# Batch zero by halves, dummy matmuls in the first gaps, folded weights in pairs of chunks, and the softmax scale moved into the input

## The chip, the cores and the metric

The kernel runs on one core of a Trainium2 chip. The metric is the device time of one execution in microseconds (us), median of several runs. The engines of the core run side by side and meet at semaphores: TensorE (PE, matmuls; PEld is its weight load), VectorE (DVE), ScalarE (ACT), GpSimd (POOL, which here also issues the loads) and SyncE (SP, which issues the stores).

## The reference

Two attentions in a row, and then a two-layer network with a squared ReLU. The shapes are 8 batches, 8 heads, 576 tokens, 32 packed queries, head size 64; the network has width 512 and an inner width of 2048.

```python
def sm_attn(qq, kk, vv):
    s = scale * np.matmul(qq, kk.transpose(0, 1, 3, 2))     # scale = 1/8
    s = s - np.max(s, axis=-1, keepdims=True)
    a = np.exp(s)
    a = a / (np.sum(a, axis=-1, keepdims=True) + 1e-09)
    return np.matmul(a, vv)
p_packed = sm_attn(p, k, v)             # 32 packed queries read 576 tokens
out = sm_attn(q, p_packed, p_packed)    # 576 tokens read the 32 packed results
x = out.transpose(0, 2, 1, 3).reshape(B * S, H * D)
h = x @ w_in
g = np.maximum(h, 0.0) ** 2
return g @ w_out                        # 4608 x 512, float32
```

## The kernel before

The kernel never forms `x`. It multiplies the packed result `pp` of a batch by `w_in` once, which gives a folded weight `M` of 2 x 128 rows (two groups `qd` of four heads, 32 packed entries each) by 2048 columns. Layer one then is `M` times the normalised weights `a2` of the second attention. The steps of one batch, by their names in the plan:

| step | what it does |
|---|---|
| Lk, Lv, Lq | loads of keys, values, queries, cast to bf16 on the way (issued by GpSimd) |
| Tk, Tq | transposes on VectorE |
| S1, PV | scores and context of the packed queries; XT copies them out (`pp`, `rD` = 1/denominator, `pq`) |
| M | folded weights, four chunks of 512 columns |
| S2, N | scores of the second attention, exponential, sum, log, inverse, product (`a2`) |
| R | layer one and ReLU, 16 blocks of 128 of the inner width |
| F1 | square (into `gT`); F2 | layer two, in tiles of 128 tokens |

A list scheduler in the kernel (`Plan`) puts the steps of all batches in an order at build time, with a time for each piece and a count of buffers for each pool. Each engine runs its instructions in that order. The parts that matter here (cuts are marked):

```python
    def fills(self, gap, t):          # dummy matmuls for a planned gap of TensorE
        return 0
...
        def keep_clock(ps):
            for _ in range(plan.fill):
                nc.tensor.matmul(ps, lhsT=idle_b[:, :P], rhs=idle_b, start=True, stop=True)
...
            def dma_kq(self, name, qd):       # all of one group's keys or queries
                t = getattr(self, name + "b")[qd] = qkv.tile([P, JT * D], BF16, name=name + "_b", tag="kqb")
                nc.gpsimd.dma_start(t, src[self.b, qd * QH:(qd + 1) * QH].rearrange("h (a j) d -> (h a) (j d)", j=JT))
            def tr_q(self, qd):
                nc.vector.transpose(
                    self.qT[:, qd].rearrange("p dh (j a) -> p j dh a", a=32),
                    self.t.qb[qd][:].rearrange("p (j dh dl) -> p j dh dl", dh=2, dl=32))
...
            def m(self, c):
                pss = [ps_att.tile([P, 512], F32, name="ps_a", tag="a") for _ in range(NQD)]
                keep_clock(pss[0][:, :256])
                for h in range(QH):
                    for qd in range(NQD):
                        pr, e = divmod(h, 2)
                        o = 32 * (h ^ qd)
                        nc.tensor.matmul(pss[qd][o:o + 32, :], lhsT=self.pp[64 * e:64 * e + 64, qd * P + pr * 64 + 32 * (e ^ qd):][:, :32],
                                         rhs=w_in_b[64 * e:64 * e + 64, qd * 2 + pr, c * WCH:(c + 1) * WCH], start=True, stop=True)
            def m_out(self, c, e, eng):
                if eng is nc.scalar:
                    nc.scalar.activation(dst, self.psm[c][e], ACT.Copy, scale=self.rD[:, e:e + 1])
                else:
                    nc.vector.tensor_scalar_mul(dst, self.psm[c][e], self.rD[:, e:e + 1])
...
            def n_mul(self, qd, hf):
                nc.vector.tensor_tensor(out=self.a2[:, qd, n0:n1].rearrange("p (c n) -> p c n", n=HALF),
                                        in0=self.e2[qd, hf], in1=self.ls[qd, hf], op=ALU.mult)
...
        def f1_mm(a, fb):
            ps = ph[a.b, fb] = ps_h.tile([P, 2, 512], F32, name="ps_h", tag="h")
            for qd in range(NQD):
                for c in range(2):
                    nc.tensor.matmul(ps[:, c, :HALF], lhsT=a.M[:, qd, fb * FB:(fb + 1) * FB],
                                     rhs=a.a2[:, qd, c * HALF:(c + 1) * HALF], start=(qd == 0), stop=(qd == NQD - 1))
...
        WIDE = tuple(range(B))      # batches whose second attention runs on all 576 tokens at once
        ld = load_steps(0) + w_in_load() + w_out_load()[:2] + load_steps(1) + w_out_load()[2:]
```

PSUM has three pools of two tiles each: `ps_a` (one bank a tile: S1, PV, M), `ps_h` (two banks a tile: S2, N, layer one) and `ps_o` (layer two).

Of the kernel before, what the change touches and what calls it, by code (L numbers as in the profile page):

```python
# [10 lines left out]
ALU = mybir.AluOpType  # L11
# [37 lines left out]
class Plan:  # L49
# [232 lines left out]
        return best[1]  # L282

    def fills(self, gap, t):
        return 0


def kernel_impl(tc, q, k, v, p, w_in, w_out, out):
# [15 lines left out]
    with ExitStack() as ctx:  # L304
# [4 lines left out]
        att = ctx.enter_context(tc.tile_pool(name="att", bufs=2))  # L309
        small = ctx.enter_context(tc.tile_pool(name="small", bufs=3))  # L310
        mpool = ctx.enter_context(tc.tile_pool(name="mpool", bufs=2))
        rpool = ctx.enter_context(tc.tile_pool(name="rpool", bufs=3))
        opool = ctx.enter_context(tc.tile_pool(name="opool", bufs=3))
        ps_att = ctx.enter_context(tc.tile_pool(name="ps_att", bufs=2, space=bass.MemoryType.PSUM))
        ps_h = ctx.enter_context(tc.tile_pool(name="ps_h", bufs=2, space=bass.MemoryType.PSUM))
# [34 lines left out]
                eng.tensor_copy(dst, src)  # L350

        def setup():
            nc.vector.memset(pT_bd[0][:, :BDW + 2 * P], 0.0)
            nc.vector.memset(ones_c[:, :1], 8.0)
            nc.vector.memset(ones_c[:64, 1:2], 8.0)
            nc.vector.memset(ones_c[64:, 1:2], 0.0)
            nc.vector.memset(kT[:, :, GM * P + 64:], 0.0)
            nc.vector.memset(v_t[0][64:, :, GM * D:], 0.0)
            nc.vector.memset(v_t[1][64:, :, GM * D:], 0.0)
            nc.vector.memset(pq_bd[0][:, :BDW + 2 * P], 0.0)  # L360

        def setup_rest():
            nc.gpsimd.memset(ones_bd, 0.0)
            for h in range(QH):
                nc.gpsimd.memset(ones_bd[32 * h:32 * h + 32, 32 * h:32 * h + 32], 0.125)
            nc.gpsimd.memset(pT_bd[1][:, :BDW + 2 * P], 0.0)
            nc.gpsimd.memset(pq_bd[1][:, :BDW + 2 * P], 0.0)
            nc.gpsimd.memset(idle_b, 0.0)

        def keep_clock(ps):  # L370
            for _ in range(plan.fill):
# [25 lines left out]
        class Loads:  # L397
# [5 lines left out]
            def dma_kq(self, name, qd):  # L403
                src = {"k": k, "q": q}[name]
                t = getattr(self, name + "b")[qd] = qkv.tile([P, JT * D], BF16, name=name + "_b", tag="kqb")
                nc.gpsimd.dma_start(t, src[self.b, qd * QH:(qd + 1) * QH].rearrange("h (a j) d -> (h a) (j d)", j=JT))  # L406

            def dma_v(self, i, h0, h1):
                n = GM + 1 if i < 2 else GM
                src = v[self.b, h0:h1].rearrange("h (a j) d -> a h (j d)", j=JT)  # L410
                nc.gpsimd.dma_start(self.vr[32 * i:32 * i + 32, h0:h1, :n * D], src[:, :, J0[i] * D:(J0[i] + n) * D])  # L411
# [13 lines left out]
        class Att:  # L425
# [8 lines left out]
                    setattr(self, name, pool.tile(shape, dt, name=name, **kw))  # L434
                return getattr(self, name)

            def tr_q(self, qd):
                self.tile_of("qT", att, [P, NQD, 2, S], BF16, bufs=1)
                nc.vector.transpose(  # L439
                    self.qT[:, qd].rearrange("p dh (j a) -> p j dh a", a=32),  # L440
                    self.t.qb[qd][:].rearrange("p (j dh dl) -> p j dh dl", dh=2, dl=32))

            def tr_k(self, qd):
                for i, n in (0, GM + 1), (2, GM):
# [68 lines left out]

            def m(self, c):
                self.tile_of("M", mpool, [P, NQD, DFF], BF16)
                pss = [ps_att.tile([P, 512], F32, name="ps_a", tag="a") for _ in range(NQD)]
                keep_clock(pss[0][:, :256])
                for h in range(QH):
                    for qd in range(NQD):
                        pr, e = divmod(h, 2)  # L520
                        o = 32 * (h ^ qd)
                        nc.tensor.matmul(pss[qd][o:o + 32, :], lhsT=self.pp[64 * e:64 * e + 64, qd * P + pr * 64 + 32 * (e ^ qd):][:, :32],  # L522
                                         rhs=w_in_b[64 * e:64 * e + 64, qd * 2 + pr, c * WCH:(c + 1) * WCH],
                                         start=True, stop=True)
                self.psm[c] = pss

            def m_out(self, c, e, eng):
                dst = self.M[:, e, c * WCH:(c + 1) * WCH]
                if eng is nc.scalar:
                    nc.scalar.activation(dst, self.psm[c][e], ACT.Copy, scale=self.rD[:, e:e + 1])  # L530
                else:
                    nc.vector.tensor_scalar_mul(dst, self.psm[c][e], self.rD[:, e:e + 1])  # L532

            def ps_s(self, hf):
                if hf is None:
# [38 lines left out]
            def n_mul(self, qd, hf):  # L574
                self.tile_of("a2", att, [P, NQD, S], BF16)
                n0 = 0 if hf is None else hf * HALF
                n1 = S if hf is None else n0 + HALF
                nc.vector.tensor_tensor(out=self.a2[:, qd, n0:n1].rearrange("p (c n) -> p c n", n=HALF),  # L578
                                        in0=self.e2[qd, hf], in1=self.ls[qd, hf], op=ALU.mult)

        gT = consts.tile([P, NFB, 2 * S], BF16, name="gT")

# [2 lines left out]
        def f1_mm(a, fb):  # L585
            ps = ph[a.b, fb] = ps_h.tile([P, 2, 512], F32, name="ps_h", tag="h")
            keep_clock(ps[:, 0, :256])
            for qd in range(NQD):
                for c in range(2):
                    nc.tensor.matmul(ps[:, c, :HALF], lhsT=a.M[:, qd, fb * FB:(fb + 1) * FB],  # L590
                                     rhs=a.a2[:, qd, c * HALF:(c + 1) * HALF],
                                     start=(qd == 0), stop=(qd == NQD - 1))

        def f1_relu(a, fb, eng):
            if (a.b, fb // 2) not in rr:
# [56 lines left out]
        def cast_alt(n, engs, fn):  # L652
            return [(NAME[id(e)], COST[NAME[id(e)]][0] + n * COST[NAME[id(e)]][1] / 1000, lambda e=e: fn(e)) for e in engs]

        plan = Plan({"a": 2, "h": 2, "o": 2, "dl": 8, "p": 1, "pb": 2, "kqb": NKQ, "v": 2, "e2": 3, "r": 3,
                     "osb": 3, "ls": 2})


# [5 lines left out]
        def stage(*pieces):  # L664
            return list(pieces)
# [5 lines left out]
        def load_steps(b):  # L671
            def kq(nm, qd):
                return load_step(f"L{nm}.{b}.{qd}", 0.56, 1.5, lambda: L[b].dma_kq(nm, qd), [("kqb", 1)])

            def vv(p, n):
                h0, h1 = p * H // n, (p + 1) * H // n
                return [load_step(f"Lv.{b}.{p}.{i}", 0.6, (0.82 if i < 2 else 0.66) / n,
                                  lambda i=i: L[b].dma_v(i, h0, h1), [("v", 1)] if p == 0 and i == 0 else [])
                        for i in range(4)]

            return [kq("k", 0), kq("k", 1)] + vv(0, 1) + [kq("q", 0), kq("q", 1)]

        def w_in_load():
# [11 lines left out]
        def tr_steps(b, nm):  # L695
            if b == 0:
                old = []
            elif nm == "k":
                old = [f"S1.{b - 1}.{i}" for i in range(3)]
            else:  # L700
                old = [f"S2.{b - 1}.{qd}.{hf}" for qd, hf in halves(b - 1)]
            us = 0.84 if nm == "k" else 1.37
            return [Step(f"T{nm}.{b}.{qd}", [stage([("DVE", us, lambda qd=qd: (T[b].tr_k if nm == "k" else T[b].tr_q)(qd))])],
                         [f"L{nm}.{b}.{qd}"] + old, (), [("kqb", 0, f"L{nm}.{b}.{qd}")]) for qd in QDS]

# [21 lines left out]
                         [f"PV.{b}.1"], (), [("a", 2, f"PV.{b}.0")])]  # L727

        def m_steps(b):
            return [Step(f"M.{b}.{c}",  # L730
                         [stage([("PE", 0.43, lambda c=c: T[b].m(c))]),
                          stage(*[[("ACT", 0.69, lambda c=c, e=e: T[b].m_out(c, e, A)),
                                   ("DVE", 0.74, lambda c=c, e=e: T[b].m_out(c, e, V))] for e in QDS])],
                         [f"XT.{b}/2.0"] + [f"LWI.{c}.{i}" for i in range(2)], [("a", 2)], [("a", 1, None)])
                    for c in range(NWC)]

        def halves(b):
            return [(qd, None) for qd in QDS] if b in WIDE else QH2

        def s2_steps(b):  # L740
            res = []
# [2 lines left out]
            for qd, hf in halves(b):  # L744
                res.append(Step(f"S2.{b}.{qd}.{hf}",
                                [stage([("PE", 0.26 * m, lambda qd=qd, hf=hf: T[b].s2(qd, hf))]),
                                 stage([("ACT", 0.73 if wide else 0.49, lambda qd=qd, hf=hf: T[b].s2_exp(qd, hf))])],
                                [f"XT.{b}/2.{i}" for i in range(3)] + [f"Tq.{b}.{qd}"] + (["Z"] if b == 0 else []),
                                [(pool, 1), ("e2", 1)], [(pool, 1, None)]))
                res.append(Step(f"N.{b}.{qd}.{hf}",  # L750
                                [stage([("PE", 0.13 * m, lambda qd=qd, hf=hf: T[b].n_sum(qd, hf))]),
# [8 lines left out]

        def f1_steps(b):
            res = []
            for fb in range(NFB):
                st = [stage([("PE", 0.49, lambda fb=fb: f1_mm(T[b], fb))]),
                      stage([("ACT", 0.65, lambda fb=fb: f1_relu(T[b], fb, A))]
                            + ([("DVE", 0.75, lambda fb=fb: f1_relu(T[b], fb, V))] if b < NDV else []))]
                deps = [f"M.{b}.{fb // 4}"] + [f"N.{b}.{qd}.{hf}" for qd, hf in halves(b)]
                res.append(Step(f"R.{b}.{fb}", st, deps, [("h", 1)] + ([("r", 1)] if fb % 2 == 0 else []), [("h", 1, None)]))
            return res

# [64 lines left out]
                        [f"LP.{b0}"], [("pb", 1)], [("p", 0, f"LP.{b0}"), ("pb", 1, None)])  # L835

        NDV = 1
        NB_ACTQ = -1
        WIDE = tuple(range(B))
        ROUNDS = 1  # L840
        SEEDS = ()
        setup()
        plan.base.update(DVE=2.5, POOL=0.8, ACT=0.5, SP=0.3, DMA=1.2, PE=3.6)
        plan.stream(0, [pload(0, 2)])
        ld = load_steps(0) + w_in_load() + w_out_load()[:2] + load_steps(1) + w_out_load()[2:]
        for b in range(2, B):
            ld += load_steps(b)[:2] + ([pload(2, B)] if b == 2 else []) + load_steps(b)[2:]
        plan.stream(0, ld)
        plan.stream(0.5, [Step("Z", [stage([("POOL", 2.6, setup_rest)])], ["Lq.0.1/1.0"])])
        plan.stream(1, [pprep(0, 2), pprep(2, B)])  # L850
        plan.stream(3.5, sum([v_steps(b) for b in range(B)], []))
        plan.stream(1.5, [x_step(b) for b in range(B)])
# [55 lines left out]
```

The softmax here doesn't subtract the row's maximum and nothing guards it: scores larger than these inputs give would overflow.

## Time and profile before

| | |
|---|---|
| time, median of 3 | 255.87 us (255.71 to 257.02) |
| profiled execution | span 255.2 us |
| first matmul of the kernel | 7.00 us |
| last matmul, about | 251.4 us |
| TensorE waits for v_b (context of batch 0) | 1.4 us |
| TensorE waits for pq_bd (scores of batch 0) | 3.2 us |
| TensorE waits for w_out_b loads | 1.0 us |
| TensorE waits for pT_bd on GpSimd | 0.9 us |

How to read it: the busy shares of the page say which engine may be the bound, the stages say where it stands idle, and the timeline and the chain of waits say for what. [...]

### The profile page before, as it was taken

What the parts mean: (1) busy time and instruction counts of PE and PEld (TensorE: products, weight loads), DVE (VectorE), ACT (ScalarE), POOL (GpSimd) and SP (SyncE); (2) the same over time, 40 slices, a digit from 0 to 9 for tenths busy, and PEclk for the clock granted to TensorE, in tenths of its full rate; (3) what the DMA queues carried; (4) which work ended last, traced back from release to release, by engine and by line L of the source; (5) the groups of instructions that cost most, each with busy time, mean ns of one, the idle gap of its engine ahead of it and who ended that gap; (6) DMA issues with size and microseconds to landing.
All of it is one profiled execution on the core that took longest, in us unless ns stands there. A gap on an engine that the chain in (4) does not pass through costs nothing.

```text
span 255.2 us, 4833 instructions
## 1 busy us (share of the span) xinstructions
PE 235.5 (92%) x1856; PEld 136.5 (53%) x1856; DVE 147.1 (58%) x260; ACT 158.4 (62%) x281; POOL 58.9 (23%) x121
## 2 busy tenths in 40 slices
PE   0647998989999999999999999999999999999994
PEld 0523664565565575467436763567446645644453
DVE  5557897879989977787675768453345304500000
ACT  2237887778789778578856876677746734611110
POOL 7884563487442055103000000000000000000000
PEclk9997999999999999999999999999999999999999
DMA  6999999999999449917221111110221122122233
GB/s 113 197 198 206 204 206 205 208 229 207 203 220 204 88 82 204 223 32 110 58 52 41 44 41 45 41 41 12 55 62 42 41 59 68 41 66 71 71 82 82
DMA packets 26870, 28.42 MB, mean 111 GB/s; under 512 B 5728, under 2 KB 18272, under 8 KB 26848
## 3 DMA queue, kind: packets, MB, share of 16 engines
q0 software_dynamic: 19216, 18.55, 45.4%
q1 hardware_dynamic: 6912, 9.32, 13.6%
q10 hardware_dynamic: 720, 0.26, 0.4%
q8 instruction: 14, 0.23, 0.3%
q14 instruction: 8, 0.07, 0.1%
HBM read 37.22 MB, written 9.44 MB: 183 GB/s over the span
## 4 chain that ended last, share of the span: by engine, by line
PE 70%; DMA 19%; POOL 3%; SPq 3%; ACT 2%; issue 1%; DVE 1%; POOLq 0%
PE ps_o L637 38%; PE ps_h L590 20%; DMA p_b<-in_p_dram 5%; DMA k_b<-in_k_dram 4%; DMA out_dram<-o_sb 4%; DMA w_out_b<-in_moe_w_out_dram 3%; PE ps_a L522 3%; DMA q_b<-in_q_dram 3%; SPq L646 3%; PE ps_s L552 2%; PE ps_a L456 2%; ACT o_sb L348 2%; PE ps_pp L491 1%; PE ps_s L564 1%; POOL v_r L411 1%
## 5 line engine op out<-in xcount | busy, mean ns | idle before, releaser
L637 PE MATMUL ps_o<-w_out_b,gT 128*128 128x512 bf16 x560 | 143.1, 379 | 1.1 <-DMA w_out_b<-in_moe_w_out_dram 1.0
L600 ACT ACTIVATE r<-ps_h 128x576 bf16<-128x576 f32 x126 | 80.2, 650 | 26.1 <-PE ps_h L590 21.4
L590 PE MATMUL ps_h<-a,M 128*128 128x288 bf16 x512 | 80.7, 289 | 0.2 <-ACT r L600 0.2
L637 PEld LDWEIGHTS <-gT 128*128 128x128 bf16 x560 | 53.1, 98 | 51.0 <-issue 6.9
L607 DVE TENSOR_TENSOR gT<-r 128x1152 bf16<-128x1152 bf16 x64 | 46.8, 750 | 32.0 <-ACT r L600 16.2
L590 PEld LDWEIGHTS <-M 128*128 128x128 bf16 x512 | 49.2, 99 | 26.4 <-issue 1.9
L532 DVE TENSOR_SCALAR M<-ps_a,rD 128x512 bf16<-128x512 f32 x36 | 26.5, 748 | 17.8 <-PE ps_a L522 17.6
L348 ACT COPY o_sb<-ps_o 128x512 f32<-128x512 f32 (+1 forms) x22 | 12.6, 574 | 38.0 <-DMA out_dram<-o_sb 25.2
L350 DVE COPY o_sb<-ps_o 128x512 f32<-128x512 f32 (+1 forms) x15 | 10.0, 668 | 31.1 <-PE ps_o L617 26.9
L530 ACT ACTIVATE M<-ps_a,rD 128x512 bf16<-128x512 f32 x28 | 19.0, 688 | 7.4 <-PE ps_a L522 7.4
L411 POOL DMA_DIRECT2D v_r<-in_v_dram x32 | 18.7, 591 | 18.1 <-DVE gT L607 10.6
L439 DVE STREAM_TRANSPOSE qT<-q_b 128x1152 bf16<-128x1152 bf16 x16 | 22.0, 1372 | 0.3 <-DMA q_b<-in_q_dram 0.2
L456 PE MATMUL ps_a<-pT_bd,kT 128*128 128x128 bf16 x128 | 9.6, 230 | 8.3 <-DVE kT L445 7.4
L522 PE MATMUL ps_a<-w_in_b,pp 64*32 64x512 bf16 x256 | 14.4, 402 | 1.6 <-DVE M L532 1.1
L445 DVE STREAM_TRANSPOSE kT<-k_b 128x320 f32<-128x320 f32 (+1 forms) x32 | 13.2, 454 | 4.2 <-PE ps_a L470 2.2
L463 ACT ACTIVATE e<-ps_a 128x512 bf16<-128x512 f32 x16 | 8.9, 596 | 9.3 <-PE ps_a L456 9.3
L456 PEld LDWEIGHTS <-kT 128*128 128x128 bf16 x128 | 8.5, 103 | 10.1 <-DVE kT L445 7.6
L406 POOL DMA_DIRECT2D q_b<-in_q_dram x16 | 8.9, 561 | 21.4 <-DVE qT L439 15.1
L559 ACT ACTIVATE e<-ps_s,rD 128x576 bf16<-128x576 f32 x16 | 11.2, 737 | 4.0 <-PE ps_s L552 4.0
L552 PE MATMUL ps_s<-qT,pq_bd 128*128 128x288 bf16 x64 | 10.5, 305 | 3.2 <-ACT pq_bd L348 3.2
L578 DVE TENSOR_TENSOR a<-e,ls 128x576 bf16<-128x576 bf16 x16 | 11.7, 749 | 2.0 <-ACT ls L572 2.0
L348 ACT COPY pq_bd<-pp 32x64 bf16<-32x64 bf16 x32 | 7.7, 241 | 7.4 <-DVE pp L350 6.9
(49 smaller groups left out, 144.0 us busy)
## 6 DMA issues: line engine op xcount, KB each, us to landing
out_dram<-o_sb SPq DMA_DIRECT2D x140, 64.0 KB, 1.7
k_b<-in_k_dram POOLq DMA_DIRECT2D x16, 288.0 KB, 8.6
q_b<-in_q_dram POOLq DMA_DIRECT2D x16, 288.0 KB, 8.3
v_r<-in_v_dram POOLq DMA_DIRECT2D x16, 160.0 KB, 7.8
v_r<-in_v_dram POOLq DMA_DIRECT2D x16, 128.0 KB, 7.9
w_in_b<-in_moe_w_in_dram POOLq DMA_DIRECT2D x8, 256.0 KB, 8.4
w_out_b<-in_moe_w_out_dram POOLq DMA_DIRECT2D x8, 256.0 KB, 9.2
p_b<-in_p_dram POOLq DMA_DIRECT2D x1, 192.0 KB, 12.1
```

What stands on the lines that cost most here:

```text
L348: nc.scalar.copy(dst, src)
L411: nc.gpsimd.dma_start(self.vr[32 * i:32 * i + 32, h0:h1, :n * D], src[:, :, J0[i] * D:(J0[i] + n) * D])
L439: nc.vector.transpose(self.qT[:, qd].rearrange("p dh (j a) -> p j dh a", a=32), self.t.qb[qd][:].rearrange("p (j dh dl) -> p j dh dl", dh= ...
L456: nc.tensor.matmul(ps[:, g * P:(g + 1) * P], lhsT=self.kT[:, qd, g * P:(g + 1) * P].bitcast(BF16).rearrange("p (t two) -> p two t", two=2) ...
L522: nc.tensor.matmul(pss[qd][o:o + 32, :], lhsT=self.pp[64 * e:64 * e + 64, qd * P + pr * 64 + 32 * (e ^ qd):][:, :32], rhs=w_in_b[64 * e:64 ...
L530: nc.scalar.activation(dst, self.psm[c][e], ACT.Copy, scale=self.rD[:, e:e + 1])
L532: nc.vector.tensor_scalar_mul(dst, self.psm[c][e], self.rD[:, e:e + 1])
L552: nc.tensor.matmul(ps[:, c], lhsT=self.pq[:, blk(qd, dh)], rhs=self.qT[:, qd, dh, n0:n0 + HALF], start=(dh == 0), stop=(dh == 1))
L590: nc.tensor.matmul(ps[:, c, :HALF], lhsT=a.M[:, qd, fb * FB:(fb + 1) * FB], rhs=a.a2[:, qd, c * HALF:(c + 1) * HALF], start=(qd == 0), sto ...
L600: nc.scalar.activation(dst, src, ACT.Relu)
L607: eng.tensor_tensor(out=gT[:, fb - 1:fb + 1, o:o + S], in0=r, in1=r, op=ALU.mult)
L637: nc.tensor.matmul(po[t], lhsT=gT[:, fb, n0:n0 + P], rhs=w_out_b[:, fb, :], start=(fb == 0), stop=(fb == NFB - 1))
```

## The change

- Batch 0's queries are loaded and transposed in two halves of 288 tokens, the first half ahead of the first loads of `w_in`, the second after two of them. Its second attention and layer one run by halves too, so that the first half can start before the second is there.
- Dummy matmuls are put into planned gaps of TensorE in the first 26 us of the plan. [...] Their operand is zeroed as the first thing on VectorE, no longer last on GpSimd.
- From batch 1 on (`MPAIR`), M is built two chunks at a time, in two tiles of `ps_h` instead of `ps_a`, and copied out 1024 columns at a time.
- The factor `rD` goes from the copies of M into the product that makes `a2`, so that M need not wait for it.
- The ReLU buffers grow from three to four. The scheduler makes a new order from all this.

The core of the diff (cuts are marked; `f1_mm_half`, `f1_relu_half` and the plan's steps for halves follow the same pattern):

```diff
     def fills(self, gap, t):
-        return 0
+        if t > 26.0 or gap < 0.6:
+            return 0
+        return int((gap - 0.3) / (0.214 if t < 9.0 else 0.11))
...
-        rpool = ctx.enter_context(tc.tile_pool(name="rpool", bufs=3))
+        rpool = ctx.enter_context(tc.tile_pool(name="rpool", bufs=4))
...
         def setup():
+            nc.vector.memset(idle_b, 0.0)
...
-            nc.gpsimd.memset(idle_b, 0.0)
...
+            def dma_q_half(self, qd, hf):
+                if hf == 0:
+                    self.qb[qd] = qkv.tile([P, JT * D], BF16, name="q_b", tag="kqb")
+                w = JH * D
+                nc.gpsimd.dma_start(self.qb[qd][:, hf * w:(hf + 1) * w], q[self.b, qd * QH:(qd + 1) * QH].rearrange(
+                    "h (a j) d -> (h a) (j d)", j=JT)[:, hf * w:(hf + 1) * w])
...
-            def tr_q(self, qd):
+            def tr_q(self, qd, hf=None):
+                j0, j1 = (0, JT) if hf is None else (hf * JH, (hf + 1) * JH)
                 nc.vector.transpose(
-                    self.qT[:, qd].rearrange("p dh (j a) -> p j dh a", a=32),
-                    self.t.qb[qd][:].rearrange("p (j dh dl) -> p j dh dl", dh=2, dl=32))
+                    self.qT[:, qd, :, j0 * 32:j1 * 32].rearrange("p dh (j a) -> p j dh a", a=32),
+                    self.t.qb[qd][:, j0 * D:j1 * D].rearrange("p (j dh dl) -> p j dh dl", dh=2, dl=32))
...
             def m(self, c):
-                pss = [ps_att.tile([P, 512], F32, name="ps_a", tag="a") for _ in range(NQD)]
+                pair = self.b >= MPAIR
+                if pair:
+                    pss = [ps_h.tile([P, 2, 512], F32, name="ps_m", tag="h") for _ in range(NQD)]
+                    cs = (2 * c, 2 * c + 1)
+                else:
+                    pss = [ps_att.tile([P, 512], F32, name="ps_a", tag="a").unsqueeze(1) for _ in range(NQD)]
+                    cs = (c,)
...
             def m_out(self, c, e, eng):
-                if eng is nc.scalar:
-                    nc.scalar.activation(dst, self.psm[c][e], ACT.Copy, scale=self.rD[:, e:e + 1])
-                else:
-                    nc.vector.tensor_scalar_mul(dst, self.psm[c][e], self.rD[:, e:e + 1])
+                w = 2 * WCH if self.b >= MPAIR else WCH
+                cast(eng, self.M[:, e, c * w:(c + 1) * w].rearrange("p (i n) -> p i n", n=WCH), self.psm[c][e])
...
-                nc.vector.tensor_tensor(out=self.a2[:, qd, n0:n1].rearrange("p (c n) -> p c n", n=HALF),
-                                        in0=self.e2[qd, hf], in1=self.ls[qd, hf], op=ALU.mult)
+                nc.vector.scalar_tensor_tensor(out=self.a2[:, qd, n0:n1].rearrange("p (c n) -> p c n", n=HALF),
+                                               in0=self.e2[qd, hf], scalar=self.rD[:, qd:qd + 1], in1=self.ls[qd, hf],
+                                               op0=ALU.mult, op1=ALU.mult)
...
-        WIDE = tuple(range(B))
+        MPAIR = 1
+        SPLIT = (0,)
+        WIDE = tuple(b for b in range(B) if b not in SPLIT)
...
-        ld = load_steps(0) + w_in_load() + w_out_load()[:2] + load_steps(1) + w_out_load()[2:]
+        ld = load_steps(0)[:-2] + w_in_load()[:2] + load_steps(0)[-2:] + w_in_load()[2:] + w_out_load()[:2] + load_steps(1) + w_out_load()[2:]
```

## The prediction

> **What bounds the kernel now.** I first read the busy shares, because they say which engine can set the end:
>
> ```profile
> PE 235.5 (92%) x1856; PEld 136.5 (53%) x1856; DVE 147.1 (58%) x260; ACT 158.4 (62%) x281; POOL 58.9 (23%) x121
> ```
>
> TensorE is the only candidate. Then I cut its time into stages (columns: stretch, its length, PE busy and matmuls, clock, DMA share, GB/s):
>
> ```profile
> 7.00:12.75 5.75, 3.99 (x50) 1.00 1.24 200
> 12.75:15.96 3.21, 0.00 (x1) 1.00 1.21 193
> 15.96:22.57 6.61, 5.01 (x36) 0.98 1.24 204
> 22.57:25.60 3.03, 3.03 (x25) 0.50 1.25 209
> 25.60:52.44 26.84, 24.57 (x214) 1.00 1.28 207
> 52.44:251.42 198.98, 198.95 (x1539) 1.00 0.45 91
> ```
>
> From 52.44 us on there is no gap. So only two things can move the end: the start, and the TensorE time of the work itself. Third, the timeline of the start, beside the same instruction later:
>
> ```profile
> 13.44 1.38 DVE L439 STREAM_TRANSPOSE qT<-q_b 128x1152 bf16<-128x1152 bf16 x1
> 14.74 0.39 DVE L350 CAST pp<-ps_pp 128x256 bf16<-128x256 f32 x1
> 15.96 2.13 PE L552 MATMUL ps_s<-qT,pq_bd 128*128 128x288 bf16 x8 [3.21 <-ACT pq_bd L348]
> ...
> 38.41 1.14 PE L552 MATMUL ps_s<-qT,pq_bd 128*128 128x288 bf16 x8
> ```
>
> The last matmul of the packed context ends at 12.75, but its copy to pp starts at 14.74, because two query transposes (12.03 to 14.82) stand ahead of it on VectorE. And eight score matmuls take 2.13 us here against 1.14 us later: TensorE runs at about half speed. By durations this lasts from 7.0 to about 25.6; the clock column shows it only from 22.57, so for the time before I trust the durations. Fourth, a matmul group that builds M costs something at its entry:
>
> ```profile
> 46.83 0.38 PE L637 MATMUL ps_o<-w_out_b,gT 128*128 128x512 bf16 x1
> 47.04 0.65 PE L590 MATMUL ps_h<-a,M 128*128 128x288 bf16 x4
> 47.53 0.38 PE L637 MATMUL ps_o<-w_out_b,gT 128*128 128x512 bf16 x1
> 47.84 0.41 PE L522 MATMUL ps_a<-w_in_b,pp 64*32 64x512 bf16 x8
> 48.19 0.39 PE L637 MATMUL ps_o<-w_out_b,gT 128*128 128x512 bf16 x1
> ```
>
> An output matmul before a layer-one group holds TensorE for 0.21 us (46.83 to 47.04), before an M group for 0.31 us (47.53 to 47.84): 0.10 us per entry. The M group itself holds it for 0.35 us. Last, the waits up to 52.44. The chain shows what the first S1 of batch 2 hangs on:
>
> ```profile
> 36.99 12.09 DMA p_b<-in_p_dram
> ...
> 50.43 0.60 POOL v_r L411
> ...
> 51.07 0.28 POOL pT_bd L350
> ...
> 52.44 0.61 PE ps_a L456 x8
> ```
>
> The packed queries of the later batches land at 49.1; then GpSimd issues two key loads and a value load before it expands them.
>
> [...] dense from 22.15, full speed at about 25.6. [...] Here 256 columns took 0.425 us and 512 took 0.685 us from PSUM, so about 0.16 us is fixed. [...]
>
> **The change, part by part.** Warm TensorE cost of one matmul, from dense stretches: output 0.216 us (9.06/42), 288 columns 0.1225 us (0.98/8), M group 0.35 us, S1 0.056 us (0.89/16). The instruction order of both kernels lets me add up what stands before a point.
>
> *Start.* Loads k, v keep their place, so S1 still starts at 7.0 and v lands at about 10.6. Query half 0 lands about 0.7 us before a whole load would: some 11.2 and 12.0. VectorE then does one v copy instead of two (the other goes to ACT), two half transposes (0.7 us each, half of 1.38), done at about 12.7, and is free for pp. That takes 2.0 us out. But 79 dummy matmuls of 256 columns come in, and a dummy in the queue holds up what stands behind it if it starts late or runs cold (0.21 us cold, 0.11 us warm). 14 stand before the context matmuls. They need the buffer of the last S1 exponential, so they start at about 10.2. Two cases:
> - Clock full at 12.0 (TensorE busy from 8.5 on): 8 cold and 6 warm dummies, context matmuls 12.6 to 13.4, pp, pq done at 14.9. 18 dummies end at 15.3, M chunk 0 at 15.7, its two ACT evictions at 16.4 and 17.0, 11 dummies at 17.7, the scores at 18.2.
> - Clock full only at 15.4: 14 cold dummies to 13.2, context to 14.7, 18 dummies to 17.0, scores at 19.9.
>
> Scores came at 15.96 to 18.1 before, because M chunk 0 and its evictions now stand ahead of them. Then the half scores: ACT does per half and group exp 0.49, log 0.41, exp 0.43 (the plan's sizes, in line with 0.74, 0.65, 0.68 for whole ones). The second normalised group of half 0 needs about 3.7 us on ACT and VectorE, and one more sum on TensorE stands before layer one: its start is 22.2 or 23.9, against 22.57 before. So halving brings little here by itself. At 22.57 the old kernel has 4.8 us of warm work behind it, but then runs 3 us at half speed; the new one has 3.9 us, warm. At 25.7 I get 6.3 us for the first case against 6.6 us: even, at best.
>
> *25.6 to 52.44.* The old kernel is idle for 26.84 - 24.57 = 2.3 us here: 0.9 us on the expansion shown above, 0.8 us on a w_out load at 43.3, the rest in small waits. In the order of the new kernel 30.3 us of warm work stand before the first S1 of batch 2, against 29.6: 0.75 us more. GpSimd expands one DMA issue sooner (about 1.2 us), so the gate is at about 51.2. First case: S1 at about 51.8, ahead by 0.64 + 0.75 = 1.4 us. Second: about 52.8, ahead by 0.4. Mean 0.9 us.
>
> *Pairs of chunks.* In the order there are 31 entries into M groups before and 18 after; behind the S1 of batch 2 it is 24 and 12. 12 x 0.10 = 1.2 us off a TensorE that has no gap there. This I count in full. Evictions: 36 x 0.748 + 28 x 0.688 = 46.2 us before. After: 8 single at about 0.63 and 28 double at about 1.1 (VectorE 0.685 + 2 x 0.26, ACT 0.584 + 2 x 0.21): 36 us. 10 us less for two engines busy at 60%: beside other work, so worth nothing directly.
>
> *Scale in the input.* M is copied without the scale; the same factor goes into the a2 product, still one pass per tile: 14 x 0.75 + 4 x 0.46 against 16 x 0.75. Zero. It also lets M start after the pp copy, without the reciprocal: 0.15 us, once per batch, hidden.
>
> *New waits.* A pair takes both ps_h tiles, which layer one and the scores use as well. I charge 0.4 us.
>
> Sum: 0.9 + 1.2 - 0.4 = 1.7 us off 255.87, 254.2 us.
>
> **Rivals.**
> - *Dummies in the way.* The clock turns late or the gaps are shorter than assumed, and the 14, 18 and 11 dummies push the chain. For it: 43 of them stand directly before the critical steps, 4.6 us warm or 9.2 us cold. Against: the old chain loses 2 us there anyway. Time: 255.5 to 257.
> - *ps_h becomes the bound.* 14 pairs, each about 0.7 us of matmuls plus 1.2 us of eviction in which layer one can't start; 0.5 us lost per pair would be 7 us: 261. Against: 7 to 9 output matmuls (1.5 to 1.9 us) stand behind nearly every pair.
> - *Hidden behind transfers.* DMA queues move 200 GB/s without a pause up to 52 us, so what the start gains is waited away at w_out or p_b. Then only the entries count: 254.7.
> - *Warm from the first.* If even S1 and the context run warm and the gaps close, layer one starts about 20.5: 252.
>
> **Range and chances.** The cases of the start span 1 us, the entries are fairly sure, ps_h can cost 1 to 2 us: 252.0 to 256.4 holds it 8 times in 10. Faster by over 2% means below 250.75, which needs the last rival and more: 0.04. Slower by over 2% needs ps_h as the bound: 0.03. Within 2%: 0.93.
>
> **What would show it.** Right: matmuls of 288 columns at 0.12 us from the first score on; pp at about 13.5 to 14.8; layer one's first matmul at 22 to 24; first S1 of batch 2 at 51 to 53 with the wait for its expansion gone or smaller; 0.1 us less at each joined entry; no gap after 53. Wrong: scores after 20; TensorE gaps named "ACT M" or "DVE M" behind the pairs; a dense stretch that isn't shorter though entries are fewer.

## The result, and the profile after

The changed kernel takes 253.06 us (median of 4; 252.49 to 253.85) against 256.16 us (median of 4) for the kernel before in the same runs: a ratio of 0.9877, 95% interval 0.9838 to 0.9916. That is 3.1 us less, within 2%.

The busy shares first; 79 of the 1935 matmuls are dummies:

```profile
PE 239.6 (95%) x1935; PEld 143.6 (57%) x1935; DVE 143.5 (57%) x249; ACT 158.4 (63%) x275; POOL 61.7 (24%) x122
```

TensorE's stages, with the columns of the table before and the limits of its first five rows (stretch, length, PE busy and matmuls, clock, DMA share, GB/s):

```profile
7.00:12.75 5.75, 5.33 (x58) 1.00 1.28 185
12.75:15.96 3.21, 2.91 (x41) 1.00 1.22 204
15.96:22.57 6.61, 4.61 (x35) 1.00 1.24 204
22.57:25.60 3.03, 3.01 (x31) 1.00 1.25 207
25.60:52.44 26.84, 25.52 (x232) 1.00 1.28 208
```

From 7 to 16 us TensorE is filled, but with dummies. They are there for its clock: between 22.57 and 25.60 it was 0.50 before and is 1.00 now. Between 15.96 and 22.57 TensorE is even less busy than before, and between 25.6 and 52.44 its idle time went from 2.3 to 1.3 us. The timeline of the start:

```profile
13.28 0.38 DVE L352 CAST pp<-ps_pp 128x256 bf16<-128x256 f32 x1
...
15.72 1.07 ACT L350 CAST M<-ps_a 128x512 bf16<-128x512 f32 x2 [1.03 <-PE ps_a L539]
...
16.36 1.36 PE L374 MATMUL ps_a<-idle_b 128*128 128x256 bf16 x11 [0.70 <-ACT M L350]
...
17.56 0.65 PE L566 MATMUL ps_a<-qT,pq_bd 128*128 128x288 bf16 x4
...
20.42 0.93 PE L374 MATMUL ps_a<-idle_b 128*128 128x256 bf16 x7 [0.58 <-ACT e L573]
...
22.18 0.93 PE L374 MATMUL ps_a<-idle_b 128*128 128x256 bf16 x7 [0.47 <-ACT e L573]
...
23.06 1.14 PE L615 MATMUL ps_h<-a,M 128*128 128x288 bf16 x8
```

pp comes 1.5 us sooner (14.74 before), and matmuls run at full speed from 10.6 us on: ten dummies hold TensorE for 1.09 us from 10.76 to 11.85, where three at 7.73 still held it for 0.64 us. Yet the scores start at 17.56 (15.96 before) and layer one at 23.06 (22.57 before). The third line says why in part: the eleven dummies wait for a copy of M, run when it is done, and the scores stand behind them.

Next is TensorE from 44 us on: a pair of chunks, the first S1 of batch 2, and the last group of matmuls, with that of the kernel before below it. An output matmul is on record with 0.38 us, but in a dense stretch the next one starts 0.216 us after it; so what a matmul holds TensorE for is read from start to start.

```profile
44.05 1.24 PE L671 MATMUL ps_o<-w_out_b,gT 128*128 128x512 bf16 x5
45.22 0.63 PE L539 MATMUL ps_m<-w_in_b,pp 64*32 64x512 bf16 x16
45.78 3.19 PE L671 MATMUL ps_o<-w_out_b,gT 128*128 128x512 bf16 x14
...
52.38 1.05 PE L466 MATMUL ps_a<-pT_bd,kT 128*128 128x128 bf16 x16 [0.37 <-POOL pT_bd L352]
...
244.59 3.66 PE L651 MATMUL ps_o<-w_out_b,gT 128*128 128x256 bf16 x32
```

```profile
247.76 3.66 PE L617 MATMUL ps_o<-w_out_b,gT 128*128 128x256 bf16 x32
```

Five output matmuls take 1.08 us and the pair starts at 45.22, so the entry is 0.09 us. The pair then holds TensorE until 45.78, for 0.56 us; two single chunks held it for 2 x 0.35 us. S1 of batch 2 starts at 52.38, the same moment as before (52.44). So in this profile nearly the whole gain lies behind that point: from there to the last group of matmuls it is 192.2 us against 195.3 us. The point itself varies: in two experiments below that keep the order, it lies at 51.57 and 51.22.

That 3.1 us divides like this. The new order has done 8 more output matmuls (1.73 us) and 8 fewer of layer one (0.98 us) by that point: 0.75 us. The 24 chunks of M left then held TensorE for 24 x 0.346 = 8.3 us, now 12 x 0.56 = 6.7 us: 1.6 us. 12 entries fewer at 0.09 us: 1.1 us. That makes 3.5 us; 0.4 us went into something else, of which the profile names 0.3 us, a wait for gT.

### The profile page after: what moved, and what is told of

Same layout as the page of the kernel before. It is cut to its first block, busy times and chain, and to the rows that moved or that the text cites. A ratio compares the mean times of both kernels' runs of the same rounds, so it can differ in the third digit from the quotient of the medians.

```text
span 252.1 us, 4976 instructions
## 1 busy us (share of the span) xinstructions
PE 239.6 (95%) x1935; PEld 143.6 (57%) x1935; DVE 143.5 (57%) x249; ACT 158.4 (63%) x275; POOL 61.7 (24%) x122
## 4 chain that ended last, share of the span: by engine, by line
PE 69%; DMA 20%; POOL 5%; SPq 1%; issue 1%; DVE 1%; ACT 1%; DVEq 0%; ACTq 0%; POOLq 0%
PE ps_o L671 40%; PE ps_h L605 19%; DMA v_r<-in_v_dram 6%; DMA p_b<-in_p_dram 5%; DMA k_b<-in_k_dram 4%; DMA w_out_b<-in_moe_w_out_dram 3%; PE ps_m L539 3%; PE ps_s L566 2%; DMA out_dram<-o_sb 2%; PE ps_a L466 2%; POOL w_in_b L428 2%; SPq L680 1%; PE ps_pp L501 1%; PE ps_s L578 1%; POOL v_r L420 1%
## 5 line engine op out<-in xcount | busy, mean ns | idle before, releaser
L634 ACT ACTIVATE r<-ps_h 128x576 bf16<-128x576 f32 x112 | 70.9, 649 | 25.8 <-PE ps_h L605 22.4
L605 PE MATMUL ps_h<-a,M 128*128 128x288 bf16 x448 | 71.1, 286 | 0.0
L352 DVE CAST M<-ps_m 128x1024 bf16<-128x1024 f32 x14 | 17.1, 1224 | 11.6 <-PE ps_m L539 11.6
L449 DVE STREAM_TRANSPOSE qT<-q_b 128x1152 bf16<-128x1152 bf16 (+1 forms) x18 | 21.9, 1232 | 3.2 <-DMA q_b<-in_q_dram 3.1
L350 ACT CAST M<-ps_m 128x1024 bf16<-128x1024 f32 x14 | 14.2, 1012 | 6.5 <-PE ps_m L539 6.4
L592 DVE SCALAR_TENSOR_TENSOR a<-e,rD,ls 128x576 bf16<-128x576 bf16 (+1 forms) x18 | 13.1, 745 | 4.5 <-ACT ls L586 4.3
L352 POOL COPY pT_bd<-pT 32x128 bf16<-32x128 bf16 x28 | 10.0, 358 | 13.9 <-PE ps_a L480 12.4
L408 POOL DMA_DIRECT2D k_b<-in_k_dram x16 | 8.7, 544 | 15.9 <-DVE kT L455 6.5
L374 PE MATMUL ps_a<-idle_b 128*128 128x256 bf16 x59 | 9.1, 306 | 3.2 <-ACT e L573 1.4
L374 PEld LDWEIGHTS <-idle_b 128*128 128x128 bf16 x79 | 8.3, 107 | 6.4 <-issue 3.9
```

The source lines that it names most:

```text
L350: nc.scalar.copy(dst, src)
L449: nc.vector.transpose(self.qT[:, qd, :, j0 * 32:j1 * 32].rearrange("p dh (j a) -> p j dh a", a=32), self.t.qb[qd][:, j0 * D:j1 * D].rearra ...
L592: nc.vector.scalar_tensor_tensor(out=self.a2[:, qd, n0:n1].rearrange("p (c n) -> p c n", n=HALF), in0=self.e2[qd, hf], scalar=self.rD[:, q ...
L634: nc.scalar.activation(dst, src, ACT.Relu)
```

## The experiments

My theory after the result: the pairs bring the gain, each by one entry and one exit of the 64x32 groups (the time lost ahead of such a group and behind it); the start brings little, since loads cap it, first of all at the gate, the point where the first S1 of batch 2 waits for the expanded packed queries. Rivals: the warm clock, the halves, the wider copies or the new order. Ratios are to the kernel before in the same runs.

**No dummies.** `fills` returns 0; the order of the rest is unchanged.

```diff
-        if t > 26.0 or gap < 0.6:
+        if True:
             return 0
```

> The changed kernel without any dummy matmul, its order of instructions otherwise the same. Theory (pairs carry most of the gain, the start is capped by the gate at 52.4 us where the first S1 of batch 2 waits for the packed queries): TensorE stays at half speed until about 26 us, layer one starts about 1 us later than 23.1, and the first S1 of batch 2 slips from 52.4 to about 53; time 253.6 to 254.4. Rival (the warm clock carries the gain): 255.5 or more.

253.35 us, ratio 0.9868 (0.9841 to 0.9896). No loss can be told from zero. Layer one starts at 21.18, 1.9 us sooner than with dummies where I had expected 1 us later, though at half speed: its first eight matmuls take 2.12 us, against 1.14 us with dummies. Full speed shows from 23.24 on, where an M group of eight is on record with 0.41 us. What the dummies win in clock they take in delay.

**No pairs.**

```diff
-        MPAIR = 1
+        MPAIR = B
```

> The changed kernel with single chunks of M in every batch, all else kept (the scheduler makes a new order). Theory: the pairs are worth 2.3 us, in 0.10 us at each of 12 entries saved and 0.13 us less for each pair's matmuls; time 255.0 to 255.8, entries 0.1 us each again. Rival (the start carries the gain): 253.8 or less.

256.22 us, ratio 0.9986 (0.9966 to 1.0005): with halves, dummies, scale and fourth buffer, but without pairs, no gain can be told from zero. The time is 0.4 us above my range: from 0.9877 to 0.9986 the pairs are worth about 2.8 us, not 2.3. Entries from an output matmul cost 0.094 us again (median of 18).

**The old kernel with pairs.** Pairs from batch 1 on and the scale in the input, as in the diff above, in the kernel before; nothing else.

> The kernel before with pairs of chunks from batch 1 on and the scale in the input, nothing else (whole batch 0, no dummies, three ReLU buffers). Theory: 2.3 us off the kernel before, 253.5 to 254.4. Rival (the start carries the gain): 255.5 or more. Rival (ps_h becomes the bound without the fourth ReLU buffer): over 256.2, with gaps of TensorE behind the pairs.

253.88 us, ratio 0.9883 (0.9854 to 0.9911): the gain is there without halves, dummies or fourth ReLU buffer. The scale alone has 0.9974 in the old kernel (below), so 2.3 us of it are the pairs'. No bound on ps_h shows.

**The old kernel with dummies alone.** `fills` as in the diff, the memset of idle_b moved to the front of VectorE.

> The kernel before with the dummy matmuls alone (84 of them by its own planned gaps, the zeroed operand first on VectorE), its order otherwise the same. Theory: the start gets warm and some 1 to 1.5 us shorter, but S1 of batch 2 stays at 52.4 us behind the packed queries, and the old order has no more work to put before it; time 255.7 to 256.2. Rival (the warm clock carries the gain): 254.5 or less.

256.68 us, ratio 0.9993 (0.9977 to 1.0009), no gain and 0.5 us above my range. The start runs at full speed (eight scores in 1.14 us at 17.50, against 2.13 us before), but it isn't shorter: layer one begins at 23.74 instead of 22.57, and S1 of batch 2 at 52.39; its wait for the packed queries grew from 0.9 to 1.4 us.

**Batch 0 whole.** The changed kernel with `SPLIT = ()` and the old order of loads.

```diff
-        SPLIT = (0,)
+        SPLIT = ()
...
-        ld = load_steps(0)[:-2] + w_in_load()[:2] + load_steps(0)[-2:] + w_in_load()[2:] + w_out_load()[:2] + load_steps(1) + w_out_load()[2:]
+        ld = load_steps(0) + w_in_load() + w_out_load()[:2] + load_steps(1) + w_out_load()[2:]
```

> The changed kernel with batch 0 whole again (queries loaded, transposed and used whole, the old order of loads), pairs, scale in the input, dummies by its own gaps and four ReLU buffers kept. Theory (the halves bring nothing, the pairs all): 252.8 to 253.7, as the changed kernel. Rival (the halves are worth what the earlier first layer one is worth): 254 or more.

253.59 us, ratio 0.9887 (0.9858 to 0.9917), layer one at 23.04. The halves bring nothing that can be told from zero.

**Dummies in a bank of their own.** They write a tile of ps_o instead of the next step's.

```diff
+        idle_ps = []
...
             for _ in range(plan.fill):
-                nc.tensor.matmul(ps, lhsT=idle_b[:, :P], rhs=idle_b, start=True, stop=True)
+                if not idle_ps:
+                    idle_ps.append(ps_o.tile([P, NE], F32, name="ps_idle", tag="o"))
+                nc.tensor.matmul(idle_ps[0][:, :256], lhsT=idle_b[:, :P], rhs=idle_b, start=True, stop=True)
```

> The changed kernel, same order and number of dummies, but they write a tile of ps_o, which nothing else uses before 29 us, instead of the tile of the step that follows. Theory A: a dummy that writes the buffer of the next step can't run in the gap, since the gap is the wait for that buffer; it runs after it and delays the step (1.2 us before the scores, 0.76 us twice before later ones). In its own tile it runs in the gap: scores at about 16.4 instead of 17.56, first layer one at 20.5 to 21.5 instead of 23.06, at full clock. And the gate: S1 of batch 2 still at 52.2 to 52.5, its wait for the expanded packed queries longer by about 1 to 2 us, time 252.7 to 253.4. Rival (the start is not capped): S1 of batch 2 at about 50.5 to 51, time 251.2 to 252.

253.33 us, ratio 0.9875 (0.9854 to 0.9896). Its timeline, with what ended each wait in brackets:

```profile
15.77 1.38 PE L378 MATMUL ps_idle<-idle_b 128*128 128x256 bf16 x11
...
16.98 0.65 PE L570 MATMUL ps_a<-qT,pq_bd 128*128 128x288 bf16 x4
...
20.93 1.14 PE L619 MATMUL ps_h<-a,M 128*128 128x288 bf16 x8
```

```profile
31.12 0.62 PE L470 MATMUL ps_a<-pT_bd,kT 128*128 128x128 bf16 x8 [0.66 <-DVE kT L459]
34.93 0.29 PE L505 MATMUL ps_pp<-e,v_b 128*128 128x64 bf16 x4 [1.55 <-DVE v_b L352]
```

The dummies now run inside the gap, with no wait, and layer one starts 2.1 us sooner at full clock (eight matmuls in 1.14 us). And then TensorE waits 0.66 us for batch 1's keys and 1.55 us for its values: 2.2 us, the whole of it. S1 of batch 2 is at 52.27. The cap is there, but not where I had put it: batch 1's own loads take the gain before the packed queries can.

**Packed queries loaded early**, ahead of the last six w_out loads, alone and with the dummies in their own bank.

```diff
-        ld = load_steps(0)[:-2] + w_in_load()[:2] + load_steps(0)[-2:] + w_in_load()[2:] + w_out_load()[:2] + load_steps(1) + w_out_load()[2:]
+        ld = load_steps(0)[:-2] + w_in_load()[:2] + load_steps(0)[-2:] + w_in_load()[2:] + w_out_load()[:2] + load_steps(1) + [pload(2, B)] + w_out_load()[2:]
...
-            ld += load_steps(b)[:2] + ([pload(2, B)] if b == 2 else []) + load_steps(b)[2:]
+            ld += load_steps(b)
```

> The changed kernel with the load of the later packed queries ahead of the last six w_out loads instead of behind the keys of batch 2. Theory (gate): the wait of S1 of batch 2 for the expansion goes, S1 of batch 2 at 51 to 52, time lower by 0.3 to 1 us, 252.2 to 252.9. Rival (the w_out loads come later in its place and their wait grows from 0.7 us by as much): 253.0 to 253.8.

> Both: dummies in a tile of ps_o and the packed queries early. Theory (start delayed by dummies, then capped by the gate): both together bring more than the sum of each, S1 of batch 2 at 50 to 51, time 251.0 to 252.2. Rival (other loads cap it as well: keys and values of batch 2, w_out): 252.4 or more, with TensorE waiting on loads between 30 and 52 us.

254.48 us, ratio 0.992 (0.990 to 0.994), and 254.14 us, ratio 0.990 (0.9878 to 0.9922). S1 of batch 2 starts at 47.1 and 47.5 and no longer waits for the packed queries. But the scheduler has also moved it: some 30 output matmuls and 64 of layer one stand before it, against 49 and 80 in the changed kernel, about 6 us less work. So no time is won: by their ratios the two lie 1.1 and 0.6 us above the changed kernel (0.9877), the second within the noise. The idle time between 25.6 and 52.44 grows from 1.3 us to 2.5 and 4.5 us. My theory of this one gate fell, and the rival's general form held, though not its detail. The named waits of TensorE in that stretch, first in the one, then in the other: an M pair for VectorE's copy of pp, 0.9 us in both; S1 for the transposed keys, 0.8 and 1.7 us; layer one for the ReLU's buffer, 0.4 and 0.6 us; layer two for w_out, 0.3 and 0.8 us. So no single gate replaces the packed queries: several chains are late together.

**A pair broken in the middle.** One matmul of the full array between the two chunks of each pair; buffers, copies and order stay.

```diff
                 for i, ch in enumerate(cs):
+                    if i == 1:
+                        nc.tensor.matmul(pss[0][:, 1, :8], lhsT=idle_b[:, :P], rhs=idle_b[:, :8], start=True, stop=True)
```

> The changed kernel with one matmul of the full array (128 weights, 8 columns) between the two chunks of each of the 14 pairs. Pairs, their buffers, their 1024-column copies and the order all stay. Theory (what is saved is one entry and one exit of the 64x32 groups per pair, 0.10 and 0.13 us): each pair holds TensorE for 0.56 + 0.23 us and a little for the extra matmul, 14 times about 0.25 to 0.3 us, time 256.0 to 257.2, all of the gain gone. Rival (the wider copies, their buffers or the new order bring the gain): at most 0.1 us per pair for the extra matmul, 253.0 to 254.4.

256.16 us, ratio 0.9983 (0.9971 to 0.9996). A broken pair in its timeline:

```profile
124.72 0.81 PE L673 MATMUL ps_o<-w_out_b,gT 128*128 128x512 bf16 x3
125.47 0.41 PE L541 MATMUL ps_m<-w_in_b,pp 64*32 64x512 bf16 x8
125.81 0.18 PE L536 MATMUL ps_m<-idle_b 128*128 128x8 bf16 x1
125.92 0.41 PE L541 MATMUL ps_m<-w_in_b,pp 64*32 64x512 bf16 x8
126.26 2.33 PE L673 MATMUL ps_o<-w_out_b,gT 128*128 128x512 bf16 x10
```

It holds TensorE from 125.47 to 126.26, 0.79 us instead of 0.56: 0.34 for each half and 0.11 from the extra matmul to the second half. Twelve of the 14 pairs stand behind S1 of batch 2, and the stretch from there to the last group grows from 192.2 us to 195.0 us (51.57 to 246.61): 2.8 us, 12 x 0.23. In the ratios 2.7 us of the 3.1 us came back. This settles it: the wider copies and the new order are still there, and nearly all of the gain is gone. What in the array takes the time at entry and exit, no run here shows.

**Tile by tile.** The same 16 matmuls with the loop over the two chunks innermost.

> The changed kernel with the 16 matmuls of a pair in another order: both chunks of one tile after each other, not all eight tiles of one chunk and then all of the next. Theory (a fixed cost per group, and eight tiles that run side by side): the hold stays near 0.56 us [...], time 252.7 to 253.7. Rival [...]: the hold of a pair grows to 1 us and more, time 258 or more.

252.97 us, ratio 0.986 (0.9839 to 0.9881); a pair holds TensorE for 0.58 us. That eight tiles run side by side shows in the changed kernel: in its pair at 45.22 the eight matmuls of the first chunk, on record with 0.39 us each, all start before 45.3. Order inside the group matters little. In its profile S1 of batch 2 happens to start at 51.22 and the span is 251.2 us, against 52.38 and 252.1 us in that of the changed kernel, with otherwise the same order: here the end moves with that point.

**The scale alone, in the old kernel.** `MPAIR = B` in the old kernel with pairs.

> The kernel before with the scale moved into the product that makes a2, and nothing else (single chunks, whole batch 0, no dummies). Theory: copies of M are 0.06 to 0.1 us shorter each on engines that are not the bound; no difference, 255.8 to 256.8. Rival (M may start earlier and its copies are shorter, so this carries part of the gain): 255.3 or less.

255.74 us, ratio 0.9974 (0.996 to 0.9987): 0.7 us faster, against my expectation of none. In its profile GpSimd starts to expand the packed queries at 49.49 (51.07 before), S1 of batch 2 starts at 51.31, and the idle time between 25.6 and 52.44 is 0.75 us. Whether the shorter copies or just the new order does it isn't settled, the less so as that start moves by 1.2 us between profiles of one order. The run without pairs (0.9986, 0.9966 to 1.0005) neither shows nor excludes these 0.7 us.

**Fewer loads.** Dummies in their own bank, and six of eight w_out loads left out: layer two uses the first two over and over, so it computes something else with the same matmuls.

```diff
-            nc.tensor.matmul(po[t], lhsT=gT[:, fb, n0:n0 + P], rhs=w_out_b[:, fb, :],
+            nc.tensor.matmul(po[t], lhsT=gT[:, fb, n0:n0 + P], rhs=w_out_b[:, fb % 4, :],
...
-        ld = load_steps(0)[:-2] + w_in_load()[:2] + load_steps(0)[-2:] + w_in_load()[2:] + w_out_load()[:2] + load_steps(1) + w_out_load()[2:]
+        ld = load_steps(0)[:-2] + w_in_load()[:2] + load_steps(0)[-2:] + w_in_load()[2:] + w_out_load()[:2] + load_steps(1)
```

> The changed kernel with the dummies in their own tile, and with six of the eight w_out loads left out: layer two takes its weights from the first two over and over (fb modulo 4), so it computes something else with the same matmuls, and about 8 us of transfers are missing between 30 and 45 us. Theory (the early start is waited away because the stream of loads caps the kernel up to 52 us): S1 of batch 2 before 49 us, TensorE idle between 25.6 and 52.4 down from 3.4 us to 1.5 or less, time 250.5 to 251.8. Rival (TensorE's own work or the copies out of PSUM cap it): 252.8 or more.

258.66 us, ratio 1.0098 (1.0075 to 1.0121): slower with fewer loads, which neither theory expected. Two waits of TensorE, and then the stage they fall in:

```profile
40.16 0.65 PE L570 MATMUL ps_s<-qT,pq_bd 128*128 128x288 bf16 x4 [1.12 <-ACT M L350]
...
43.89 1.01 PE L470 MATMUL ps_a<-pT_bd,kT 128*128 128x128 bf16 x8 [1.27 <-POOL pT_bd L352]
```

```profile
40.00:52.44 12.44, 10.59 (x94) 0.73 1.22 206
```

The scheduler drew batch 2 forward, TensorE ran out of ready work near 40 us (0.7 us busy between 39 and 41), and its clock was at half from 41.0 to 47.8 us: eight S1 matmuls in 1.01 us at 43.89, against 0.62 us at 29.11 in the same run. The second wait shown came after the fall. In this new order the scores of batch 1 also wait 1.12 us for the copy of an M pair, the clash on ps_h that doesn't show in the changed kernel. The waits for batch 1's keys and values stand (0.49 and 1.01 us), for those loads come before the ones left out. So this run doesn't prove the cap by removal; that rests on the named waits of the dummies in their own bank.

## Why the prediction was right, and where it was off

The time lay in the range, 1.1 us below the centre; the gain was 3.1 us where I had 1.7. Start, entries and the charge for new waits came out near what I had summed; the missing 1.4 us is mainly one term that I did not have, the exit of the 64x32 groups.

- *Start.* pp at 13.3 (I had 13.4 in the first case), scores at 17.6 (18.2), layer one at 23.1 (22.2 to 23.9), S1 of batch 2 at 52.4 (51.8 to 52.8): close or in the range, and with them the 0.9 us, of which 0.06 + 0.75 = 0.8 us came. Part of this is luck, for two errors cancelled. The clock was full at 10.6, sooner than in either case (12.0 and 15.4, both my estimates: the trace of the kernel before doesn't show what decides that moment); but from the scores to layer one it took 5.5 us instead of 4.0, because twice seven dummies waited for an exponential and then held up the next step (with dummies in their own bank it took 3.95 us). And the gate did not move to 51.2: the expansion started 0.5 us sooner, at 50.59, but its four copies took 1.74 us instead of 1.32, and S1 still waited 0.37 us for it. The 0.75 us of work drawn forward is what came. Right also that a dummy holds up what stands behind it: the eleven at 16.36 put the scores off by 1.20 us. I reckoned with the wait of the eleven dummies for the copy of M, but didn't see that they need not wait at all; that was worth 2.1 us of start and, because of the loads, nothing at the end.
- *The step that was off in size: pairs of chunks.* I wrote "12 x 0.10 = 1.2 us" and took a pair's matmuls at "about 0.7 us". The entries cost and save what I said (0.09 us each). But while one chunk holds TensorE for 0.346 us, the second chunk of a pair adds only about 0.21 us (0.56 - 0.346); the other 0.13 us is paid once per group. By the starts it is paid at the group's end: in the pair at 45.22 the second chunk starts 0.23 us after the first, and the output matmul behind it another 0.33 us later. A pair measured 0.56 us, so 12 x 0.13 = 1.6 us was missing from the sum. With it the sum is 254.2 - 1.6 = 252.6 us; it started from 255.87 us, and the kernel before took 256.16 us in the runs of the result. That the wider copies are worth nothing directly was right: with the pairs broken they are still there, and the gain is gone.
- *New waits on ps_h.* I charged 0.4 us, and about 0.4 us is left over; but that is a coincidence in size, for behind 52.4 us the profile names 0.3 us for gT and no wait of a pair.
- *Scale in the input.* "Zero" is not shown: alone in the old kernel it brought 0.7 us; the cause isn't settled. The product with the scale took 0.81 us at 576 columns where I had put 0.75 us, which costs nothing, for VectorE isn't the bound.
- *Rivals.* "Dummies in the way" was real as a mechanism and small in time. "Hidden behind transfers" was right for the start, but with the loads of batch 1 as the first to bind. "ps_h becomes the bound" did not come. "Warm from the first" came true for layer one only with the dummies in their own bank (20.93, I had about 20.5), and there the time was 253.3 us, not 252.

*The clock of the kernel before.* I read half speed from 7.0 to about 25.6. The groups of M show otherwise:

```profile
18.02 0.63 PE L522 MATMUL ps_a<-w_in_b,pp 64*32 64x512 bf16 x8
...
20.18 0.41 PE L522 MATMUL ps_a<-w_in_b,pp 64*32 64x512 bf16 x7 [0.29 <-DVE M L532]
...
24.61 0.63 PE L522 MATMUL ps_a<-w_in_b,pp 64*32 64x512 bf16 x8
```

The groups of 0.63 us ran at half speed, the one of 0.41 us at full speed. In the trace the clock is full from 18.9, after a start at half speed (eight scores in 2.13 us at 15.96), then half from 22.3 (0.51 on average up to 25.8; eight matmuls of layer one take 2.10 us at 22.57) and full again from 25.8 (1.00). The sum used only the 3 us at half speed behind 22.57, so it doesn't change.

## What to carry to other kernels

Where TensorE has no gap, count the changes between tile shapes, not only the matmuls: here each group of 64x32 tiles cost about 0.22 us at its ends, and joining groups two by two brought 2.3 to 2.8 us of the 3.1 us. A dummy matmul needs a buffer that is free in the gap; if it writes the buffer of the step it precedes, it waits with that step and then delays it: layer one started at 23.06 us that way, and at 20.93 us with the dummies in their own bank. And before speeding up a start, look at which loads the next batch waits for: 2.1 us won there came back as 2.2 us of waits.

## What was unexpected of the hardware

- The hold of a 64x32 group of eight tiles fits 0.21 us for each 512 columns plus 0.13 us, 0.35 us for one chunk and 0.56 us for two, nearly whatever the order of its matmuls (0.58 us tile by tile).
- TensorE reached full speed at 10.6, 3.7 us after its first S1 matmul at 6.9, with a pause of 0.26 us between. Eleven dummies at 1.06 to 3.6, with 3.3 us of idleness behind them, had left it at half speed: S1 took 1.04 us for eight matmuls at 6.90, against 1.06 us for sixteen at 31.98.
- The clock fell to half after pauses of about 1 us. With loads left out TensorE was busy for 1.5 of the 3 us up to 41.0, its longest pause 1.1 us, and then had half the clock until 47.8 us. In the kernel before it was busy for 1.8 of the 3.4 us from 18.9 to 22.3, its longest pause 0.9 us, and then had half the clock until 25.8 us. With the dummies in their own bank it stayed at 1.00 from 25.6 to 40, across a wait of 1.55 us. What decides when it falls or rises, no run here shows.
